# The seam between a long convolution and a gated MLP: v kept in DRAM by chunks, loads and side work reordered

## The chip, the core and the metric

The kernel runs on one core of one Trainium2 chip. Its engines are TensorE (PE in the profile; PEld is its weight load), VectorE (DVE), ScalarE (ACT), GpSimd (POOL) and SyncE (SP), each with its own in-order list of instructions, and 16 DMA engines that they share. SP issues nearly all loads, POOL nearly all stores and the copies between buffers. The metric is the device time of one execution in microseconds (us); a time of a kernel is the median of several executions. In this document a time within the execution, such as 457.14, is counted in us from the start of the span.

## The reference, cut to what matters

The inputs are 2048 tokens of 576 channels. Two blocks follow each other, each with a layer norm in front and a residual around it (sa, ca, ga, sb, cb, gb come from a small conditioning product):

```
h = layernorm(x) * (1 + ca) + sa
x = x + ga * A(h)          # A: a state-space layer as a long causal convolution
h = layernorm(x) * (1 + cb) + sb
x = x + gb * B(h)          # B: a gated MLP

A: K[d, l] = Re sum_n C[d,n] * exp(dt*A[d,n]*l) * dt*B[d,n];  y = causal_conv(u, K) + u * Dskip
B: z = gelu(x @ w_in);  z1, z2 = halves of z;  z2 = layernorm(z2)
   g = w_sp @ z2 + b_sp;  out = (z1 * g) @ w_out
```

## The kernel before

**Convolution.** The convolution is done as a transform in stages of small matmuls. The 576 channels are cut into five chunks: four of 128 and one of 64 (`CHW`); the code calls the last two `c3` and `c4`. Per chunk the stages are `u_unit` (forward), `z_unit` (multiply by the transformed kernel), `v_unit` (inverse, first half) and `y_unit` (inverse, second half, plus the residual). A unit of u, z or v is 128 partitions by 512 values; a chunk of 128 channels has eight, the last chunk four. Between `v_unit` and `y_unit` the data change their layout by way of DRAM: `v_unit` lets ACT copy ("evict") its PSUM result to an SBUF tile `v` (two buffers), and POOL stores that to `v_d`; `y_vload` loads two halves of four token tiles back with SP, `y_xload` loads the same piece of the input x, `y_unit` multiplies, DVE adds PSUM and x in place, and POOL stores the sum to `x1_d`. There are 4 y units per chunk, numbered 0 to 3. Tiles of the names "u1", "ue", "us", "za", "zb" are used again, once their first use is over, as places for these loads. A loop over ticks interleaves all this with the making of the kernel K; it ends before the last chunks are through.

**The seam** (lines 652 to 701) is written out by hand, and its order is kept on each engine as written (`mlp.nc = mlp.tied`). It mixes the last z, v and y units with the start of the MLP: 

- `start` loads `mrow` (the two modulation rows), `x1l` (the last chunk's 64 channels of x) and part of `x1f` (the first four token tiles of x); `start_load(q)` loads block q of the gate half of `w_in` (five blocks of 512 columns; 0 and 1 were loaded in the loop).
- Each block is turned into two fp16 parts: `start_sum(q)` lets ACT sum the squares, `win_scale` has PE add these over partitions and DVE make a power of two of it (seven small instructions), `start_hi(q)` converts on ACT, `start_lo(q)` makes the remainders with three DVE instructions and frees the block's buffer.
- `start_rows` bounds the modulation rows: two squares on ACT, a maximum on DVE, a scale (`pow2_scale`), the scaling of `mrow`, a one-value Gelu that loads ACT's table ahead of time, and the product INV_IN of three scales.
- `ln2_stats`, `roots` and `ln2_rows` make the second layer norm of a token tile on DVE.

**The MLP's first phase** (`phase_a`, line 1077) goes over 16 token tiles. `turn` transposes the normed tile on PE into PSUM, `turn_hi` copies it to fp16 on ACT, `turn_lo` makes the remainder on DVE and stores `nt`; `z2_mm(b, h)` is 14 matmuls of tile b with block h. In the first tile blocks 3 and 4 are still being prepared: `start_sum(3)`, `win_scale(8)`, `start_hi(3)`, `start_lo(3)` and the same for block 4 stand between the first matmul groups. The second phase (`phase_b`) makes the other half of z, the gate and the output.

**Queues.** Each DMA takes one of eight semaphores of its queue in turn, and so waits until the DMA eight places before it on that queue has landed. An SP or POOL instruction that waits holds up all behind it.

Line 129 stands in the profile for everything that went through the recording layer (the seam and `phase_a`), so in these stretches instructions are told apart by their tiles: `wz<-wst` on ACT with 2560 values is a sum of squares, with 2048 a conversion; `wz` on DVE is a split; `xb`, `us`, `zhl` and `x1l` on DVE with `pk` are y sums (`zhl` holds `x1f`).

Of the kernel before, what the change touches and what calls it, by code (L numbers as in the profile page):

```python
# [141 lines left out]
def ssm(tc, I, x1_d, consts_s, dram, mod_d, mlp):  # L142
# [5 lines left out]
    with ExitStack() as ctx:  # L148
# [3 lines left out]
        early = ctx.enter_context(ExitStack())  # L152

        u1_d = dram.tile([2, 16, 128, D], F32, name="u1_d")
        v_d = dram.tile([128, 32, D], F32, name="v_d")
        pa_d = dram.tile([4, 6, CW], BF, name="pa_d")
        pb_d = dram.tile([4, 6, CW], BF, name="pb_d")
        pc_d = dram.tile([4, 3, CW], BF, name="pc_d")
# [294 lines left out]
        def chan(c):  # L453
            return slice(CH0[c], CH0[c] + CHW[c])
# [40 lines left out]

        def v_unit(c, i):
            za, zb = st.pop((c, i))
            v = part("v")
            pm = ps1()
            T.matmul(pm, inva, za, start=True, stop=False)  # L500
            T.matmul(pm, invb, zb, start=False, stop=True)
            A.activation(v, pm, AF.Copy)
            G.dma_start(v_d[:, kr(c, i), chan(c)], by(v, c))

        def y_vload(c, q):
            bs = slice(4 * q, 4 * q + 4)
            w = CHW[c]
            if c == NC - 1:
                t = part("ue", 4)
                vt = [t[:, :4 * w], t[:, 4 * w:]]  # L510
            elif c == NC - 2 and q < 2:
                vt = [part("za"), part("zb")]
            else:
                vt = [part("u1", 5)[:, :4 * w] for _ in range(2)]
            st["yv", c, q] = vt
            for hh in range(2):
                S.dma_start(by(vt[hh], c), v_d.rearrange("(b g r) k d -> b (g r k) d", g=4, r=2)[bs, 128 * hh:128 * hh + 128, chan(c)].rearrange("b p d -> p b d"))

        def y_xload(c, q):
            bs = slice(4 * q, 4 * q + 4)  # L520
            if c >= NC - 2 and q == 0:
                xb = mlp.x1f[:, :, chan(c)]
            elif c == NC - 1:
                xb = mlp.x1l[:, bs]
# [128 lines left out]
        mlp.nc = mlp.tied  # L653
        V, A, G, T, S = mlp.nc.vector, mlp.nc.scalar, mlp.nc.gpsimd, mlp.nc.tensor, mlp.nc.sync
        c3, c4 = NC - 2, NC - 1
        y_load(2, 2)
        mlp.start()
        mlp.start_load(2)
        mlp.start_x1()
        for i in range(2):  # L660
            z_unit(c4, i)
# [2 lines left out]
        for i in range(2):  # L664
            z_unit(c4, 2 + i)
            v_unit(c4, i)
            mlp.win_scale(5 + i, False)
            if i == 0:
                mlp.start_sum(1)
        v_unit(c4, 2)  # L670
        v_unit(c4, 3)
        for c, r in ((2, 3), (c3, 0), (c3, 1), (c3, 2), (c3, 3), (c4, 0), (c4, 1), (c4, 2), (c4, 3)):
            y_xload(c, r)
        y_unit(2, 1)
        for c, r in ((2, 3), (c3, 0), (c3, 1), (c4, 0), (c4, 1)):
            y_vload(c, r)
        mlp.start_hi(0)
        mlp.start_hi(1)
        mlp.start_lo(0)
        y_unit(2, 2)  # L680
        y_vload(c3, 2)
        mlp.start_sum(2)
        mlp.win_scale(7, False)
        mlp.start_lo(1)
        y_unit(2, 3)
        y_vload(c3, 3)
        y_vload(c4, 2)
        y_vload(c4, 3)
        mlp.start_hi(2)
        mlp.start_rows(ps2(), ps2())  # L690
        mlp.start_lo(2)
        y_unit(c3, 0)
        mlp.start_load(3)
        y_unit(c4, 0)
        mlp.ap = mlp.mc
        mlp.ln2_stats(0)
        y_unit(c3, 1)
        mlp.roots(x=0)
        for c, r in ((c4, 1), (c3, 2), (c4, 2), (c3, 3), (c4, 3)):
            y_unit(c, r)  # L700
        mlp.nc = tc.nc

# [43 lines left out]
class Mlp:  # L746
# [73 lines left out]
    def start(self):  # L820

        nc = self.nc
        V, S, I = nc.vector, nc.sync, self.I
        mc = self.mc = self.pool(self.ctx, "mc", 1)
        self.c2 = ExitStack()
        ones = self.ones = mc.tile([128, 128], F32, name="ones")
        V.memset(ones, 1.0)
        self.ident = mc.tile([128, 128], F32, name="ident")
        S.dma_start(self.ident, I["c_small"][:, :128])
        self.sc = mc.tile([128, 96], F32, name="sc")  # L830
        wzp = self.pool(self.c2, "wzp", 1)
# [3 lines left out]
        self.x1l = wzp.tile([128, 16, CHL], F32, name="x1l")  # L835
        S.dma_start(self.x1l[:, 4:], I["x"][:, 4:, D - CHL:])
# [9 lines left out]
    def start_rows(self, *ps):  # L846

        V, A, col, mrow = self.nc.vector, self.nc.scalar, self.col, self.mrow
        s0, s1 = [p[:, :, :D // 2] for p in ps]
        halves = [mrow[:, i].rearrange("p (h d) -> p h d", h=2) for i in range(2)]  # L850
        A.activation(s0, halves[0], AF.Square, accum_out=col(T0))
        A.activation(s1, halves[1], AF.Square)
        V.tensor_reduce(col(T1), s1, axis=mybir.AxisListType.XY, op=ALU.max)
# [5 lines left out]
        for q in range(5, 8):  # L859
            V.tensor_tensor(self.wcol(q, INV_IN), self.wcol(q, I_W), col(I_H), op=ALU.mult)  # L860

    def start_load(self, q, pool=None):
        n = min(512, FH - 512 * q)
# [119 lines left out]
    def ln2_stats(self, b):  # L983
        V, ap = self.nc.vector, self.ap
        if b < 4:
            self.xts[b] = self.x1f[:, b]
        else:
            V.tensor_copy(self.xts[b][:, D - CHL:], self.x1l[:, b])
# [88 lines left out]
    def phase_a(self):  # L1077
# [313 lines left out]
```

## Time and profile before

| | |
|---|---|
| median of 3 runs | 1921.5 us (1918.57 to 1923.9) |
| profiled execution | 1920.97 us, span 1919.2 us |
| PE busy | 1814.3 us, 95% of the span |
| DVE busy | 908.5 us, 47% |
| ACT busy | 636.4 us, 33% |
| POOL busy | 207.9 us, 11% |
| data moved by DMA | 290.42 MB, mean 151 GB/s |
| mean granted PE clock | 0.981 |

How to read what follows. A row of the timeline has the start in us, the duration in us, the engine (a q behind it: its sequencer, which issues), the line, the operation, the tiles as out<-in, shapes, how many instructions were merged, and in brackets the idle time of the engine before it with what ended that. An instruction's end is its start plus its duration, and on DVE and ACT the next may start a little before that. A row of a tile's view has the count, the durations in ns, and the first and last start; "DMA to landing" is the time from issue to the last byte. In a table of stretches each engine has its busy us and its instructions; then come the granted PE clock, the mean busy share of the DMA engines (over 1 where transfers overlap) and GB/s.

### The profile page before, as it was taken

To read this page: it belongs to the slowest core of one execution; us is meant where nothing else is said; L and a number is where in the kernel's file an instruction comes from. 1 tells how busy PE (TensorE), PEld (TensorE's weight loads), DVE (VectorE), ACT (ScalarE), POOL (GpSimd) and SP (SyncE) were. 2 spreads that over 40 slices of the span, in tenths; PEclk is the share of its full clock that TensorE was granted. 3 is DMA by queue.
4 is the path that set the end of the run, shared out by engine and by line. 5 is a ranking of instruction groups with operands and counts; after the bars stand their busy time and mean duration, and the time that the engine had idled before them with its cause. 6 is when DMAs were issued, how large, how long until landed. Compare 5 with 4: busy or idle time off the path is not lost.

```text
span 1919.2 us, 28165 instructions
## 1 busy us (share of the span) xinstructions
PE 1814.3 (95%) x11634; PEld 934.3 (49%) x11634; DVE 908.5 (47%) x2020; ACT 636.4 (33%) x874; POOL 207.9 (11%) x317
## 2 busy tenths in 40 slices
PE   3778999986999998999999999999999999999999
PEld 1444555654444443444466444457444447444457
DVE  5987999848999871224352121152212143211221
ACT  3768999743777552121100011110101110001000
POOL 3121223331121110000000000000000000000000
PEclk9888999997999999999999999999999999999999
DMA  8667546897565456446552233452323342223211
GB/s 218 171 176 252 133 130 169 199 273 219 188 235 188 147 185 241 165 168 212 195 176 72 87 116 121 182 179 68 108 94 137 131 174 67 105 88 114 73 59 38
DMA packets 144145, 290.42 MB, mean 151 GB/s; under 512 B 20912, under 2 KB 74672, under 8 KB 133648
## 3 DMA queue, kind: packets, MB, share of 16 engines
q1 hardware_dynamic: 111888, 141.58, 24.0%
q0 software_dynamic: 29824, 142.47, 22.2%
q10 hardware_dynamic: 2304, 4.57, 0.6%
q8 instruction: 91, 1.49, 0.3%
q14 instruction: 38, 0.31, 0.1%
HBM read 219.11 MB, written 60.02 MB: 145 GB/s over the span
## 4 chain that ended last, share of the span: by engine, by line
PE 67%; DVE 7%; issue 4%; ACT 3%; DMA 2%; POOL 1%; DVEq 0%; ACTq 0%; POOLq 0%
PE pg L1233 13%; PE pg L1234 13%; PE pg L1235 13%; PE pz L1221 11%; PE pz L129 4%; PE po L1267 3%; PE po L1268 3%; PE po L1269 3%; DVE bsz L129 1%; ACT zhl L129 1%; DMA wsst<-in_w_spT 1%; PE po L1221 1%; DMA wf<-win_d 1%; PE pk L491 1%; DVE nt L129 1%
## 5 line engine op out<-in xcount | busy, mean ns | idle before, releaser
L1233 PE MATMUL pg<-wsp,z2f 128*128 128x512 f16 x1152 | 437.2, 380 | 0.0
L1234 PE MATMUL pg<-wsp,z2f 128*128 128x512 f16 x1152 | 436.6, 379 | 0.0
L1235 PE MATMUL pg<-wsp,z2f 128*128 128x512 f16 x1152 | 436.6, 379 | 0.0
L1237 DVE SCALAR_TENSOR_TENSOR gt<-pg,sc,bsp 128x512 f32<-128x512 f32 x72 | 54.0, 750 | 632.9 <-PE pg L1235 632.9
L1241 ACT ACTIVATE z<-gt 128x512 f16<-128x512 f32 x72 | 45.3, 630 | 802.7 <-DVE gt L1239 802.7
L129 PE MATMUL pz<-wz,nt 128*128 128x512 f16 (+1 forms) x1120 | 240.4, 363 | 5.5 <-DVE nt L129 2.3
L1221 PE MATMUL pz<-n2q,wf 128*128 128x512 f16 (+1 forms) x924 | 219.5, 383 | 4.2 <-DMA wf<-win_d 4.2
L1233 PEld LDWEIGHTS <-z2f 128*128 128x128 f16 x1152 | 112.6, 98 | 142.2 <-issue 13.6
L1235 PEld LDWEIGHTS <-z2f 128*128 128x128 f16 x1152 | 112.7, 98 | 135.9
L1234 PEld LDWEIGHTS <-z2f 128*128 128x128 f16 x1152 | 112.7, 98 | 128.6
L129 PEld LDWEIGHTS <-nt 128*128 128x128 f16 x1120 | 105.2, 99 | 136.7 <-issue 45.6
L1221 PEld LDWEIGHTS <-wf 128*128 128x128 f16 x1008 | 98.0, 98 | 147.1 <-issue 35.0
L1268 PE MATMUL po<-wout,z 128*128 128x288 f16 x576 | 164.7, 286 | 0.2 <-DVE ot L1271 0.2
L1267 PE MATMUL po<-wout,z 128*128 128x288 f16 x576 | 164.8, 286 | 0.0
L1269 PE MATMUL po<-wout,z 128*128 128x288 f16 x576 | 164.7, 286 | 0.0
L1229 POOL DMA_DIRECT2D z2f<-z_d x72 | 38.7, 537 | 1071.7 <-PE pg L1235 998.0
L1270 ACT ACTIVATE ot<-po 128x288 f32<-128x288 f32 x32 | 13.1, 410 | 194.2 <-PE po L1267 187.6
L1271 DVE TENSOR_TENSOR ot<-ot,po 128x288 f32<-128x288 f32 x32 | 14.5, 453 | 131.8 <-ACT ot L1270 131.7
L1242 DVE TENSOR_TENSOR gt<-gt,z 128x512 f32<-128x512 f32 x72 | 49.7, 690 | 45.6 <-ACT z L1241 45.6
L1267 PEld LDWEIGHTS <-z 128*128 128x128 f16 x576 | 56.4, 98 | 14.9 <-issue 0.7
L1269 PEld LDWEIGHTS <-z 128*128 128x128 f16 x576 | 56.4, 98 | 14.6 <-issue 0.4
L1268 PEld LDWEIGHTS <-z 128*128 128x128 f16 x576 | 56.4, 98 | 14.2
(283 smaller groups left out, 2404.5 us busy)
## 6 DMA issues: line engine op xcount, KB each, us to landing
z2f<-z_d POOLq DMA_DIRECT2D x72, 1024.0 KB, 5.1
wsst<-in_w_spT SPq DMA_DIRECT2D x64, 512.0 KB, 4.5
wf<-win_d SPq DMA_DIRECT2D x72, 320.0 KB, 3.2
z_d<-zhl POOLq DMA_DIRECT2D x16, 1152.0 KB, 6.8
u_d<-st1o POOLq DMA_DIRECT2D x16, 576.0 KB, 4.3
u<-u_d SPq DMA_DIRECT2D x36, 256.0 KB, 4.8
us<-ue POOLq DMA_DIRECT2D x72, 128.0 KB, 4.5
v_d<-v POOLq DMA_DIRECT2D x36, 256.0 KB, 3.7
```

The lines of the kernel that those rows point to most:

```text
L129: return self.tc.keep_in_program_order(f(*a, **k))
L1221: nc.tensor.matmul(pm.rearrange("p (t c) -> p t c", t=4), w[:p, kw], self.n2[q][:p, :, kn], start=i == 0, stop=i == len(Z1) - 1)
L1229: nc.gpsimd.dma_start(z2, self.z2_d[f])
L1233: T.matmul(pm, z2[:, st, 0], w[:, 0], start=st == 0, stop=False)
L1234: T.matmul(pm, z2[:, st, 0], w[:, 1], start=False, stop=False)
L1235: T.matmul(pm, z2[:, st, 1], w[:, 0], start=False, stop=st == 15)
L1237: V.scalar_tensor_tensor(t, pm, self.qcol(q, INV_SP), self.bsp[q], op0=ALU.mult, op1=ALU.add)
L1241: A.activation(p[:, 0], t, AF.Copy)
L1242: V.tensor_tensor(t, t, p[:, 0], op=ALU.subtract)
L1267: T.matmul(pl[:, :288], p[:, 1, ts], self.wout[:, f, 0, hs], start=f == 0, stop=f == 17)
L1268: T.matmul(pa[:, :288], p[:, 0, ts], self.wout[:, f, 0, hs], start=f == 0, stop=False)
L1269: T.matmul(pa[:, :288], p[:, 0, ts], self.wout[:, f, 1, hs], start=False, stop=f == 17)
```

## The change

Four things change, all around the seam.

1. `v_d` becomes five DRAM tensors, one for each chunk, with the chunk's channels innermost. A partition of a `v` tile is then one run of 2 KB in DRAM (before: runs of 512 bytes, 256 in the last chunk). The loads read the same number of bytes in runs of the same length as before.
2. The last two v units write their evictions to tiles of the name "ue" (four buffers). The x load of y unit (2, 2) is issued after the loads of w_in block 2. Block 0's conversion stands ahead of the last two v units, block 1's after them; the splits of blocks 0 and 1 stand ahead of and between the first y units. The load of block 3 keeps its place on SP.
3. `start_rows` is divided: its two squares (`start_sums`) come early, the rest after y unit (2, 2) and ahead of the sum of squares of block 2, which now comes behind the table load on ACT; INV_IN of block 2 is made in `win_scale(7)`, which moves behind y unit (2, 3). The split of block 2 moves into `phase_a`, between `turn_hi(0)` and `turn_lo(0)`, and frees its buffer for the load of block 4 there.
4. `ln2_rows(0)` stands ahead of the last four y units instead of behind them. `x1l` loses its unused first four rows.

```diff
-        v_d = dram.tile([128, 32, D], F32, name="v_d")
+        v_d = [dram.tile([128, 32, w], F32, name="v_d") for w in CHW]
...
         def v_unit(c, i):
             za, zb = st.pop((c, i))
-            v = part("v")
+            v = part("ue", 4) if c == NC - 1 and i > 1 else part("v")
...
-            G.dma_start(v_d[:, kr(c, i), chan(c)], by(v, c))
+            G.dma_start(v_d[c][:, kr(c, i)], by(v, c))
...
+            rows = v_d[c].rearrange("(b h g) k d -> b h (g k) d", b=16, h=2)[bs].rearrange("b h p d -> p h b d")
...
-                S.dma_start(by(vt[hh], c), v_d.rearrange("(b g r) k d -> b (g r k) d", g=4, r=2)[bs, 128 * hh:128 * hh + 128, chan(c)].rearrange("b p d -> p b d"))
+                S.dma_start(by(vt[hh], c), rows[:, hh])
...
-        y_load(2, 2)
+        y_vload(2, 2)
         mlp.start()
         mlp.start_load(2)
+        y_xload(2, 2)
         mlp.start_x1()
...
+        mlp.start_hi(0)
         v_unit(c4, 2)
         v_unit(c4, 3)
...
+        mlp.start_hi(1)
+        mlp.start_lo(0)
         y_unit(2, 1)
...
-        mlp.start_hi(0)
-        mlp.start_hi(1)
-        mlp.start_lo(0)
+        mlp.start_sums(ps2(), ps2())
+        mlp.start_lo(1)
         y_unit(2, 2)
         y_vload(c3, 2)
+        mlp.start_rows()
         mlp.start_sum(2)
-        mlp.win_scale(7, False)
-        mlp.start_lo(1)
         y_unit(2, 3)
...
+        mlp.start_load(3)
+        mlp.win_scale(7)
+        y_unit(c3, 0)
+        y_unit(c4, 0)
         mlp.start_hi(2)
-        mlp.start_rows(ps2(), ps2())
-        mlp.start_lo(2)
-        y_unit(c3, 0)
-        mlp.start_load(3)
-        y_unit(c4, 0)
         mlp.ap = mlp.mc
         mlp.ln2_stats(0)
         y_unit(c3, 1)
         mlp.roots(x=0)
-        for c, r in ((c4, 1), (c3, 2), (c4, 2), (c3, 3), (c4, 3)):
+        y_unit(c4, 1)
+        mlp.ln2_rows(0)
+        for c, r in ((c3, 2), (c4, 2), (c3, 3), (c4, 3)):
             y_unit(c, r)
...
+    def start_sums(self, *ps):
+        A, mrow = self.nc.scalar, self.mrow
+        s0, self.sq = [p[:, :, :D // 2] for p in ps]
+        halves = [mrow[:, i].rearrange("p (h d) -> p h d", h=2) for i in range(2)]
+        A.activation(s0, halves[0], AF.Square, accum_out=self.col(T0))
+        A.activation(self.sq, halves[1], AF.Square)
...
         V.tensor_scalar(mrow, mrow, col(S_H), None, op0=ALU.mult)
+        for q in range(5, 7):
+            V.tensor_tensor(self.wcol(q, INV_IN), self.wcol(q, I_W), col(I_H), op=ALU.mult)
         A.activation(col(T0), self.ones[:, :1], AF.Gelu_apprx_tanh)
...
             if b == 1:
                 self.ln2_stats(1)
                 self.roots(x=1)
-            self.ln2_rows(b)
+                self.ln2_rows(1)
             if b == 0:
                 self.turn(0)
                 self.turn_hi(0)
+                self.start_lo(2)
                 self.start_load(4)
                 self.x1_load(4)
                 self.turn_lo(0)
```

More of the change, by code (lines that the diff above doesn't have):

```diff
@@ L507, in y_vload @@
             w = CHW[c]
+            rows = v_d[c].rearrange("(b h g) k d -> b h (g k) d", b=16, h=2)[bs].rearrange("b h p d -> p h b d")
             if c == NC - 1:
                 t = part("ue", 4)
-                vt = [t[:, :4 * w], t[:, 4 * w:]]
-            elif c == NC - 2 and q < 2:
+                st["yv", c, q] = t[:, :4 * w], t[:, 4 * w:]
+                for hh in range(2):
+                    S.dma_start(by(t[:, 4 * w * hh:4 * w * hh + 4 * w], c), rows[:, hh])
+                return
+            if c == NC - 2 and q < 2:
                 vt = [part("za"), part("zb")]
@@ L523, in y_xload @@
             elif c == NC - 1:
-                xb = mlp.x1l[:, bs]
+                xb = mlp.x1l[:, 4 * q - 4:4 * q]
             else:
@@ L834, in start @@
         self.wz = wzp.tile([128, 10, FH], F16, name="wz")
-        self.x1l = wzp.tile([128, 16, CHL], F32, name="x1l")
-        S.dma_start(self.x1l[:, 4:], I["x"][:, 4:, D - CHL:])
+        self.x1l = wzp.tile([128, 12, CHL], F32, name="x1l")
+        S.dma_start(self.x1l, I["x"][:, 4:, D - CHL:])
         self.xz = self.pool(self.c2, "xz", 1)
@@ L844, in start_x1, with start_rows @@
         self.nc.sync.dma_start(self.x1f[:, :, :384], self.x1_d[:4, :, :384].rearrange("b p d -> p b d"))
-    def start_rows(self, *ps):
-        V, A, col, mrow = self.nc.vector, self.nc.scalar, self.col, self.mrow
[L849 to L853, printed above, removed]
+    def start_sums(self, *ps):
[4 more added lines that the diff above has]
+        A.activation(self.sq, halves[1], AF.Square)
+    def start_rows(self):
+        V, A, col, mrow = self.nc.vector, self.nc.scalar, self.col, self.mrow
+        V.tensor_reduce(col(T1), self.sq, axis=mybir.AxisListType.XY, op=ALU.max)
         V.tensor_scalar(col(T1), col(T1), 1152.0, None, op0=ALU.mult)
@@ L987, in ln2_stats @@
         else:
-            V.tensor_copy(self.xts[b][:, D - CHL:], self.x1l[:, b])
+            V.tensor_copy(self.xts[b][:, D - CHL:], self.x1l[:, b - 4])
         x = self.xts[b]
```

2 lines of the change are left out of this document (removed).

## The prediction

> **What bounds the kernel now.** I read the page first (PE busy 95% of the span, DVE 47%, DMA 0.9 and over in slices 8 and 9 alone), then cut the span where the change lies, at the seam between the convolution and the gated MLP. Columns: stretch, PE, PEld, DVE, ACT, POOL busy, granted clock, DMA share, GB/s.
>
> ```profile
> 405.00:430.00 25.00, 20.12 (x126) 13.80 (x124) 10.04 (x28) 10.85 (x12) 6.97 (x9) 0.95 1.05 315
> 430.00:457.00 27.00, 12.85 (x151) 11.73 (x151) 23.38 (x58) 8.66 (x11) 7.46 (x10) 0.69 1.02 297
> 457.00:480.00 23.00, 18.35 (x76) 8.14 (x77) 19.53 (x62) 10.04 (x14) 0.55 (x1) 0.87 0.41 137
> 480.00:700.00 220.00, 216.78 (x1067) 99.34 (x1064) 196.07 (x634) 148.16 (x185) 33.48 (x45) 1.00 0.59 195
> ```
>
> From 480 on PE is 98.5% busy: what happens there is a matter of when it starts. Between 430 and 457 PE works half of the time and DVE 87%; DMA is full from 405 to 457. So the seam is worth what DVE's in-order list there is worth, unless DMA holds it. The timeline at the end of the seam:
>
> ```profile
> 446.31 1.01 DVE L129 TENSOR_TENSOR zhl<-pk,zhl 128x512 f32<-128x512 f32 x2
> 447.04 1.97 PE L129 MATMUL pk<-u,st 128*64 128x128 f32 x16 [5.98 <-DVE zhl L129]
> 453.40 0.82 DVE L129 SCALAR_TENSOR_TENSOR n<-zhl,mvx,mrow 128x576 f32<-128x576 f32 x1
> 455.10 0.19 DVE L129 COPY n<-n 128x64 f32<-128x64 f32 x1
> 457.14 5.42 PE L129 MATMUL pz<-wz,nt 128*128 128x512 f16 x14 [0.69 <-ACT nt L129]
> 457.29 1.02 DVE L129 TENSOR_TENSOR nt<-pt,nt 128x512 f16<-128x512 f32 x2 [1.99 <-ACT nt L129]
> ...
> 469.38 0.38 PE L129 MATMUL pz<-acc,ones 128*128 128x1 f32 x2 [2.66 <-ACT wz L129]
> 478.59 6.12 PE L129 MATMUL pz<-wz,nt 128*128 128x256 f16 x24 [0.84 <-DVE wz L129]
> ```
>
> PE waits 5.98 us for the y sums on DVE. The first MLP matmul starts at 457.14, but PE then still waits for what hangs on DVE: at 469.38 for a sum of squares queued on ACT behind a conversion that needs a DVE scale, at 478.59 for DVE's last weight split. So I count to the place where DVE takes up `nt` (the low part of the first tile, 457.29): everything DVE does after it up to 478.59 is unchanged, and PE is chained to it. The end should move by what 457.29 moves by.
>
> **The change, part by part.** The chain starts on ACT and SP.
>
> ```profile
> 415.93 0.60 ACT L129 ACTIVATE v<-pk 128x512 f32<-128x512 f32 x1 [0.59 <-PE pk L129]
> 419.66 0.60 ACT L129 ACTIVATE v<-pk 128x512 f32<-128x512 f32 x1 [0.81 <-ACT wz L129]
> 424.88 0.60 ACT L129 ACTIVATE v<-pk 128x512 f32<-128x512 f32 x1 [4.62 <-DMA v_d<-v]
> 427.26 3.88 ACT L129 ACTIVATE wz<-wst,sc 128x2048 f16<-128x2048 f32 x2
> ```
>
> *Evictions of v into "ue", first conversion ahead of them.* The third v eviction of the last chunk waits 4.62 us for a store to free its buffer, and both conversions (1.94 us each, 3.88 for two) stand behind it. In the new order the first conversion follows the 419.66 eviction (some 0.5 later) and ends at 422.1 instead of 429.2; the two evictions have their own buffers.
>
> *Load of w_in block 2 in front of the x load.* SP's rows, and two v stores alone with their landing:
>
> ```profile
> 406.61 0.43 SPq L129 DMA_DIRECT2D x1l<-in_x  x1
> 413.31 0.37 SPq L129 DMA_DIRECT2D xb<-in_x  x1
> 414.29 2.66 SPq L129 DMA_DIRECT2D wst<-in_w_in  x3
> ...
> L129 POOL DMA_DIRECT2D v_d<-v x1: 762/762/762, 409.8 to 409.8; - x1
> ...
> DMA to landing us min/median/max: 5.6/5.6/5.6
> ...
> L129 POOL DMA_DIRECT2D v_d<-v x1: 896/896/896, 416.8 to 416.8; - x1
> ...
> DMA to landing us min/median/max: 8.0/8.0/8.0
> ```
>
> The x load waited until 413.31 for its buffer, and the zhl and w_in loads behind it on SP; now these go at about 407 and only the x load, the early x1 rows and the us loads are behind that wait. The price: the store issued at 409.8 (landed after 5.6, at 415.4) now stands behind the w_in load. The one store that stood so before (issued at 416.8, just behind the 414.29 load) took 8.0. The eviction at 415.93 reuses that buffer. At 5.6 it isn't held. At 8.0 it starts at 417.8; the sum of squares behind it ends 2.9 later (415.93 to 419.66-0.81) at 420.7, the next eviction and the conversion add 0.5 and 1.9: the conversion ends at 423.15. I take 422.6, the middle of two near ends. The Trainium skill, "DMA: Bandwidth & Descriptors", section "Queues, rings and completion order", says that a DMA engine takes turns between queues a packet at a time. By that rule the POOL store would not wait for SP's load, the conversion would end at 422.1 and the time come out 0.5 lower; the 8.0 above speaks against it.
>
> *DVE and the row sums.* The rows that give the steps:
>
> ```profile
> 429.29 2.35 DVE L129 SCALAR_TENSOR_TENSOR wz<-wst,sc,wz 128x2048 f16<-128x2048 f32 x1 [4.26 <-ACT wz L129]
> 432.74 0.68 DVE L129 TENSOR_TENSOR xb<-pk,xb 128x512 f32<-128x512 f32 x1
> 439.57 0.74 DVE L129 TENSOR_REDUCE sc<-ps 128x1 f32<-128x576 f32 x1
> 440.77 1.28 ACT L129 ACT_TABLE_LOAD   x1 [2.24 <-DVE sc L129]
> 442.06 0.20 ACT L129 ACTIVATE sc<-ones 128x1 f32<-128x1 f32 x1
> ...
> 431.05 2.32 ACT L129 ACTIVATE wz<-wst 128x2560 f16<-128x2560 f32 x1
> 433.51 0.58 PE L129 MATMUL pk<-acc,ones 128*128 128x1 f32 x2 [8.38 <-ACT wz L129]
> 434.03 1.97 PE L129 MATMUL pk<-u,st 128*64 128x128 f32 x16
> 434.13 0.16 DVE L129 COPY sc<-pk 128x1 f32<-128x1 f32 x1 [0.72 <-PE pk L129]
> 435.53 2.34 DVE L129 SCALAR_TENSOR_TENSOR wz<-wst,sc,wz 128x2048 f16<-128x2048 f32 x1
> ```
>
> A weight split is three DVE instructions, 3.45 us to the next (429.29 to 432.74); a y sum 0.68. New list from the conversion's end: 0.1, split 0, sum, split 1, sum: 8.36, so the row maximum starts at 430.96 (before 439.57). The two squares it needs are ACT's next work and long done. Then comes a new serial loop: the table load waits for DVE 1.20 after the maximum's start, it and the dummy take 1.49, and the third sum of squares is now queued behind them (ACT): 433.65. From its start to PE's matmul 2.46, to 436.11; behind that matmul on PE stands y sum (chunk 4, first), whose matmuls start 0.52 later and take 1.97: 438.6. DVE comes first with its scale: 0.62 to the copy, 1.40 for the seven small ones, 0.16 for the product that moved here: 438.29. During this loop DVE idles some 2 us, which the old order did not. The first zhl sum starts at 438.7 instead of 446.31: 7.6 earlier.
>
> From there to the end of the first tile's norm it was 446.31 to 455.29: 8.98, now in another order but the same instructions; 0.2 more because the second sum's matmuls (half of those 1.97) end a little after the first sum. Split 2 (3.45) comes after, so DVE takes up `nt` at 438.7+0.2+8.98+3.45 = 451.3. The 1.99 us in which DVE waited for transposes and ACT is covered: the norm is done before the last four sums, and PE and ACT turn the tile under split 2. So 457.29 becomes 451.3: 6.0 us earlier.
>
> *Loads of v.* The last must not be later than DVE.
>
> ```profile
> 433.59 3.13 SPq L129 DMA_DIRECT2D ue<-v_d  x4
> ...
> L129 POOL DMA_DIRECT2D v_d<-v x2: 885/885/885, 425.8 to 427.7; - x2
> ...
> DMA to landing us min/median/max: 5.6/5.7/5.8
> ...
> L129 SPq DMA_DIRECT2D ue<-v_d x4: 465/798/1060, 439.7 to 442.2; - x4
> ...
> DMA to landing us min/median/max: 5.5/5.9/6.5
> ```
>
> They were released at 433.59 by the landing of the last v store (issued 427.7, in 5.8); the last, issued at 442.2, landed by 447.7 (5.5 to 6.5). The last v eviction now comes at about 424 and its store at 425, so 2.7 us earlier, and the last load by 445.0. The last sum stood 0.7 (itself and a memset) ahead of 453.40, so 6.4 after 446.31; with the norm (453.40 to 455.29) now in front it comes at 438.7+0.2+6.4+1.9 = 447.2, so it is covered by about 1.5.
>
> *2-KB stores* I cost at nothing: the last chunk's stores in runs of 256 B landed in 5.6 to 5.8 beside 5.6 for one in runs of 512 B, under the same full DMA, so the run length doesn't show. Bounds: 0 to 0.3 us on the last store. The later load of w_in block 4, now issued when split 2 ends at 451, lands within 9 us and is needed about 12 later. The smaller x1l and the fewer scale products are nothing.
>
> **Sum.** Profiled execution 1920.97 (span 1919.2 and 1.8 around it) less 6.0 is 1915.0; it lies 0.5 below the median of 1921.5, so the forecast for a median is 1915.5. Half a us of it hangs on the store, up or down.
>
> **Rivals.**
> 1. *The w_in load starves the stores.* If the 409.8 store lands only with all the traffic ahead of it, at about 420 (10.2 us, over the 8.0 row), the conversion ends at 425.4 and 2.8 of the 6.0 are gone: 1918.3. For it: DMA is full. Against: the load is no longer behind another 6 us of loads.
> 2. *DMA sets the last sum.* If the v loads land no earlier than before (447.7), then matmuls 0.65, the sum 0.45, a memset 0.3 and split 2 put `nt` at 452.7: 1916.9. For it: the share of 1.02. Against: DMA isn't asked for more, and starts earlier.
> 3. *Larger gain.* The store isn't held, DVE's 2-us wait in the loop is filled: 8 us, 1913.5.
> 4. *Slower.* A store's rows now lie 16 KB apart (32x128x4 bytes), where they were 72 KB apart. If such writes collide in DRAM, all 36 stores land later.
>
> ```profile
> v_d<-v POOLq DMA_DIRECT2D x36, 256.0 KB, 3.7
> 400.73 0.78 POOL L503 DMA_DIRECT2D v_d<-v  x1 [3.52 <-ACT v L502]
> ```
>
> A v buffer returns after two stores, 9.1 us (400.73 to 409.8); a store takes 3.7. It decides from about 9 us a store; each us over that costs some 14 us over 14 pairs, so at 9.9 the gain is lost twice: 1928. The trace shows no pitch effect, so 5%. The Trainium skill, same page, section "Latency and other measured facts", has rates falling with large power-of-two row pitches (207 GB/s at 512 KiB, 103 at 4 MiB). By that rule 16 KiB is far below where it starts, and even half the rate would keep a store under 9 us; no run here shows it yet.
>
> **How the numbers follow.** A difference under 0.3% (5.8 us) is about what a measurement of this kernel can't tell from no change, so the bound for "faster" is 1915.7. The forecast case has 0.55, with its own range 1913.5 to 1917; I put 0.40 of it below the bound; its centre lies just under that, and the 2 us of waiting that I charge in the loop may be less. Larger gain 0.12. Starved stores 0.14 and late loads 0.10 fall within 0.3%. Slower 0.09: the pitch 0.05, an unseen wait 0.04. Faster 0.52, same 0.39, slower 0.09. The range 1911.5 to 1920.0 leaves out the slower cases and part of the largest gain.
>
> **What would show it.** Right: the first two weight conversions on ACT near 420 to 426 without a wait for v_d; w_in block 2 issued near 407.5; the row maximum on DVE near 431; the zhl sum near 438.7; `nt` on DVE near 451, the transposes some 3 us before; the stretch from there to the end unchanged. Wrong: an ACT wait for v_d ahead of the 415.93 eviction of more than 2 us; PE waiting for v loads at the last sums; DVE waiting more than 3 us between the row maximum and the zhl sum; v stores landing in over 9 us in the loop.

## The result

The changed kernel takes 1917.4 us at the median (1910.9 to 1922.2), the kernel before, beside it on the same chip, 1922.1 us. The ratio is 0.9975, with a 95% interval of 0.9967 to 0.9984: about 5 us, or 3 to 6, inside the 0.3% that the forecast had called no measurable change. The profiled execution took 1917.79 us (span 1916.0), where the forecast's own sum for it was 1915.0.

The stretches of the changed kernel, columns as in the forecast (stretch, PE, PEld, DVE, ACT, POOL busy, granted clock, DMA share, GB/s):

```profile
405.00:430.00 25.00, 20.65 (x136) 14.17 (x132) 16.16 (x34) 13.09 (x15) 5.68 (x10) 0.96 1.10 335
430.00:457.00 27.00, 20.05 (x168) 14.98 (x169) 21.11 (x63) 9.30 (x10) 8.06 (x11) 0.60 0.97 284
457.00:480.00 23.00, 17.76 (x75) 7.76 (x74) 19.99 (x61) 9.70 (x12) 0.55 (x1) 0.85 0.55 180
480.00:700.00 220.00, 215.78 (x1064) 98.76 (x1062) 196.05 (x629) 148.43 (x189) 34.13 (x45) 1.00 0.58 194
```

DVE's work has moved ahead of 430 (16.16 us where it was 10.04), DMA is still full from 405 to 457, and behind 480 these sums show no change.

**One number for all traces.** The seam's first eviction of v (unit (c3, 6)) starts at different times in different executions of the same code ahead of it, so every trace is read from that eviction; it is called the mark below. Here it is in the kernel before and in the changed kernel, with the long matmul group of `phase_a` that follows a wait for `nt`:

```profile
408.93 0.60 ACT L129 ACTIVATE v<-pk 128x512 f32<-128x512 f32 x1 [5.10 <-PE pk L129]
...
702.60 13.00 PE L129 MATMUL pz<-wz,nt 128*128 128x512 f16 x62 [0.65 <-DVE nt L129]
```

```profile
409.46 0.60 ACT L129 ACTIVATE v<-pk 128x512 f32<-128x512 f32 x1 [5.10 <-PE pk L129]
...
699.33 13.00 PE L129 MATMUL pz<-wz,nt 128*128 128x512 f16 x62 [0.66 <-DVE nt L129]
```

From mark to `nt` on DVE (457.29 before, 453.98 after) it is 48.36 and 44.52: 3.84 gained. From `nt` to this group it is 245.31 and 245.35, and from the group to the end of the span 1216.60 and 1216.67. In these two traces all of the gain lies between mark and `nt`. The forecast had 6.0 there.

The timeline of the changed kernel, ACT and DVE. First the part that came as foretold:

```profile
420.38 0.60 ACT L129 ACTIVATE v<-pk 128x512 f32<-128x512 f32 x1 [1.00 <-DMA v_d<-v]
420.87 1.99 ACT L129 ACTIVATE wz<-wst,sc 128x2048 f16<-128x2048 f32 x1
423.80 0.60 ACT L129 ACTIVATE ue<-pk 128x512 f32<-128x512 f32 x1 [0.45 <-PE pk L129]
430.99 0.74 DVE L129 TENSOR_REDUCE sc<-ps 128x1 f32<-128x576 f32 x1
435.51 0.69 DVE L129 TENSOR_TENSOR us<-pk,us 128x512 f32<-128x512 f32 x1 [1.22 <-PE pk L129]
436.68 0.16 DVE L129 COPY sc<-pk 128x1 f32<-128x1 f32 x1 [0.48 <-PE pk L129]
438.60 0.69 DVE L129 TENSOR_TENSOR zhl<-pk,zhl 128x512 f32<-128x512 f32 x1 [0.24 <-PE pk L129]
```

The first conversion starts 6.4 earlier than before, the wait of 4.62 for a store is one of 1.00, the row maximum stands at 430.99 and the first zhl sum at 438.60. The second part did not:

```profile
441.67 1.04 PE L129 MATMUL pk<-u,st 128*64 128x128 f32 x16
444.98 0.44 PE L129 MATMUL pk<-ue,st 128*64 128x64 f32 x2 [2.27 <-DVE n L129]
445.98 1.01 PE L129 MATMUL pk<-ue,st 128*64 128x64 f32 x13 [0.55 <-DMA ue<-v_d]
446.89 1.91 PE L129 MATMUL pk<-u,st 128*64 128x128 f32 x15
447.13 0.42 DVE L129 TENSOR_TENSOR x1l<-pk,x1l 128x256 f32<-128x256 f32 x1 [0.58 <-PE pk L129]
448.39 1.27 PE L129 MATMUL pk<-ue,st 128*64 128x64 f32 x16
448.84 0.69 DVE L129 TENSOR_TENSOR us<-pk,us 128x512 f32<-128x512 f32 x1 [1.28 <-PE pk L129]
450.53 2.35 DVE L129 SCALAR_TENSOR_TENSOR wz<-wst,sc,wz 128x2048 f16<-128x2048 f32 x1
453.98 1.00 DVE L129 TENSOR_TENSOR nt<-pt,nt 128x512 f16<-128x512 f32 x2
```

PE stands 2.27 and then 0.55 in front of y unit (c4, 2). The first wait is put down to DVE's `n`, which has nothing to do with these matmuls; the first half of (c4, 2)'s data, issued at 439.21, landed after 5.6 us at 444.85, just ahead of them. The second wait names the load. Behind them on PE stand (c3, 3), whose data are long there, and (c4, 3); DVE waits 0.58 and 1.28 for their sums. The loads on SP's queue, and the view of the last four (the row of the issues and the time to landing):

```profile
424.54 2.85 SPq L129 DMA_DIRECT2D u<-v_d  x2
427.56 0.60 SPq L129 DMA_DIRECT2D za<-v_d  x1
428.25 1.91 SPq L129 DMA_DIRECT2D zb<-v_d  x1
430.21 0.75 SPq L129 DMA_DIRECT2D za<-v_d  x1
431.01 0.71 SPq L129 DMA_DIRECT2D zb<-v_d  x1
431.96 3.84 SPq L129 DMA_DIRECT2D ue<-v_d  x4
435.89 3.22 SPq L129 DMA_DIRECT2D u<-v_d  x4
439.21 3.17 SPq L129 DMA_DIRECT2D ue<-v_d  x4
```

```profile
L129 SPq DMA_DIRECT2D ue<-v_d x4: 612/672/1013, 439.2 to 441.4; - x4
...
DMA to landing us min/median/max: 5.6/5.9/6.1
```

In the kernel before SP stood until 433.59 for a store to land. Now it waits for nothing that long: it issues one load after the other, each issue lasting 0.5 to 2.1 us. The last four are issued from 439.2 to 441.4 (before 439.7 to 442.2) and the last lands at 447.1, where the forecast had 445.0.

### The profile page after: what moved, and what is told of

It reads as the page before. It is cut to its first block, busy times and chain, and to the rows that moved or that the text cites. A ratio compares the mean times of both kernels' runs of the same rounds, so it can differ in the third digit from the quotient of the medians.

```text
span 1916.0 us, 28166 instructions
## 1 busy us (share of the span) xinstructions
PE 1817.7 (95%) x11634; PEld 935.4 (49%) x11634; DVE 908.1 (47%) x2020; ACT 636.3 (33%) x874; POOL 199.5 (10%) x317
## 4 chain that ended last, share of the span: by engine, by line
PE 69%; DVE 7%; issue 3%; ACT 3%; DMA 1%; SPq 0%; DVEq 0%; ACTq 0%
PE pg L1244 13%; PE pg L1245 13%; PE pg L1246 13%; PE pz L1232 11%; PE po L1278 4%; PE po L1280 4%; PE po L1279 4%; PE pz L129 2%; ACT zhl L129 1%; PE pk L129 1%; DVE bsz L129 1%; DVE nt L129 1%; PE po L1232 1%; PE pk L478 1%; PE pk L491 1%
```

## The experiments

Times in this table are counted from the mark of each trace. The ratio is to the kernel before, with its 95% interval; kernels without a ratio were executed once.

| kernel | mark | first conversion | first zhl sum | nt | from zhl sum to nt | ratio |
|---|---|---|---|---|---|---|
| before | 408.93 | 18.33 | 37.38 | 48.36 | 10.98 | |
| before, once more | 410.27 | 18.36 | 37.41 | 48.39 | 10.98 | |
| changed | 409.46 | 11.41 | 29.14 | 44.52 | 15.38 | 0.9975 (0.9967 to 0.9984) |
| without three x loads | 411.88 | 11.62 | 30.45 | 43.11 | 12.66 | |
| (c3, 3) ahead of (c4, 2) | 410.09 | 11.64 | 29.36 | 42.44 | 13.08 | 0.9963 (0.9951 to 0.9974) |
| that, split 2 in the seam | 411.93 | 11.45 | 29.17 | 42.25 | 13.08 | 0.9960 (0.9947 to 0.9973) |
| sum 2 ahead of the row bound | 413.30 | 11.63 | 27.26 | 43.97 | 16.71 | 0.9977 (0.9968 to 0.9986) |
| evictions back in v | 410.52 | 11.56 | 32.49 | 45.52 | 13.03 | 0.9984 (0.9974 to 0.9993) |
| x load first again | 412.53 | 11.23 | 28.95 | 44.62 | 15.67 | 0.9988 (0.9978 to 0.9998) |
| norm last again | 413.82 | 11.53 | 29.25 | 45.48 | 16.23 | 0.9992 (0.9981 to 1.0004) |
| before, v_d by chunks alone | 412.02 | 18.37 | 37.42 | 48.39 | 10.97 | 0.9999 (0.9989 to 1.0008) |
| before, evictions to ue alone | 410.47 | 11.23 | 34.09 | 45.08 | 10.99 | 0.9992 (0.9982 to 1.0002) |
| changed, waits filled | 409.38 | 11.38 | 30.21 | 39.53 | 9.32 | 0.9956 (0.9941 to 0.9971) |

From `nt` to the group of 62 matmuls all of them have 245.29 to 245.68. The gain at `nt` that a trace shows lies inside the interval of every ratio (the changed kernel: 3.84, interval 3.1 to 6.3 us).

**Is it DMA?** The x loads of three y units are left out, and POOL writes zeros there.

```diff
                 xb = by(part("us", 4) if c == NC - 2 or (c, q) == (2, 3) else part("xb"), c)
-                S.dma_start(xb, I["x"][:, bs, chan(c)])
+                if c < NC - 2:
+                    S.dma_start(xb, I["x"][:, bs, chan(c)])
+                else:
+                    G.memset(xb, 0.0)
```

> The changed kernel, where the x loads of y units (c3, 1) to (c3, 3), 256 KB each, are left out and POOL writes zeros into these tiles instead (so three sums lack x). Theory (DMA sets the last sums): at some 310 GB/s these 0.75 MB are 2.4 us of a full DMA, the last v loads of the last chunk land at 444.5 to 445.5 instead of 447.1, PE's waits of 2.27 and 0.55 in front of (c4, 2) shrink to under 1 us, and DVE takes up nt at 451.5 to 452.5 instead of 453.98. Rival (the order on SP and PE sets them, not the bytes): the loads land within 0.5 of 447.1 and nt stays at 453.5 or later.

The view of the last four loads of v, and the DVE and POOL rows of the split behind the first conversion:

```profile
L129 SPq DMA_DIRECT2D ue<-v_d x4: 577/770/1235, 438.4 to 440.7; - x4
...
DMA to landing us min/median/max: 4.6/4.8/5.3
```

```profile
427.63 1.47 POOL L129 MEMSET us<- 128x512 f32 x3
```

```profile
427.80 1.59 DVE L129 TENSOR_SCALAR wz<-wst,sc 128x512 f16<-128x512 f32 x1
```

The last load is issued 28.8 behind the mark (31.9 in the changed kernel) and lands 33.4 to 34.1 behind it (37.5 to 38.0): 3.4 to 4.6 earlier, more than the 2.4 us of its bytes. PE no longer waits for (c4, 2), and zhl sum to `nt` takes 12.66, not 15.38; the forecast's terms for it, 9.18 and 3.45, make 12.63. So what stands ahead of the last loads of v on SP's queue does set them. The run takes away both the bytes and SP's time to issue these x loads (the last load of v is issued 3.1 earlier, and then lands 0.8 to 1.0 sooner), so it doesn't tell the two apart. Counted from the changed kernel's mark, `nt` would stand at 452.57, just past the edge of what was expected, since the zeros cost something else: the DVE instruction beside POOL's memsets took 1.59 us where it takes 0.48, and the whole list up to the zhl sum is 1.3 late.

**Is it PE's order too?** The sums that wait stand ahead of one that doesn't; then the split is put into the gap as well.

```diff
-        for c, r in ((c3, 2), (c4, 2), (c3, 3), (c4, 3)):
+        for c, r in ((c3, 2), (c3, 3), (c4, 2), (c4, 3)):
             y_unit(c, r)
```

> The changed kernel, with y unit (c3, 3) in front of (c4, 2). Theory (late loads of the last chunk, and PE in order behind them): (c3, 3)'s matmuls and sum fill the wait, the last sum starts some 1.2 earlier (at 448.5), nt at 452.8 instead of 453.98; against the kernel before 0.9969. Rival (the forecast's view, DVE's list alone sets nt): no change of nt by more than 0.3, 0.9975.

`nt` comes at 42.44, 2.08 earlier than in the changed kernel, with a ratio of 0.9963. PE still waits for the loads here, for both halves of (c4, 3), the last unit.

```profile
446.33 0.30 PE L129 MATMUL pk<-ue,st 128*64 128x64 f32 x2 [0.43 <-DMA ue<-v_d]
447.09 0.68 PE L129 MATMUL pk<-ue,st 128*64 128x64 f32 x14 [0.46 <-DMA ue<-v_d]
```

The gain is larger than the 1.2 expected because DVE's waits behind the norm are all gone, and PE runs faster: 14 matmuls of (c4, 3) take 0.68 here, 16 took 1.27 in the changed kernel. The granted clock is 1.00 here; in the changed kernel it is 0.50 from 445.0 to 449.7, where the last three units run. What that costs can be read from the run below with the evictions back in `v`, which has the changed kernel's order and a clock of 1.00 in this place. Its rows of (c3, 3) and (c4, 3):

```profile
447.43 1.04 PE L129 MATMUL pk<-u,st 128*64 128x128 f32 x15
448.56 0.69 PE L129 MATMUL pk<-ue,st 128*64 128x64 f32 x16
```

The changed kernel has 1.91 and 1.27 for the same matmuls. From the third matmul of (c4, 2), the first that waited for the second load, to the end of (c4, 3) it takes 3.68, and that run 2.33: 1.35 for the clock. So the loss had three parts: loads later than thought, PE's units in order behind the first of them, and a clock of 0.50 for these units. This run changes the last two together and doesn't separate them. They may hang together: in the changed kernel the clock is 0.98 from 444 to 445 and 0.50 from 445 to 446, so it falls as PE takes up (c4, 2) after standing for 2.27. It was 0.50 there too in the three other runs in which PE stood over 1.5 us in this place (2.48, 2.15 and 1.55), and 1.00 in this run, without the x loads and with the evictions back in `v`, where no wait there reaches 1 us. In the run shown next, with waits of 0.87 and 0.57, it falls in the last unit: 1.00 from 449 to 450, 0.71 to 451, 0.50 to 452. That the standing brings it down was not tested.

```diff
-        for c, r in ((c3, 2), (c4, 2), (c3, 3), (c4, 3)):
-            y_unit(c, r)
+        y_unit(c3, 2)
+        y_unit(c3, 3)
+        mlp.start_lo(2)
+        y_unit(c4, 2)
+        y_unit(c4, 3)
...
                 self.turn_hi(0)
-                self.start_lo(2)
```

> As the run with (c3, 3) first, and the split of block 2 (3.45 us of DVE) also goes back into the seam, behind the sum (c3, 3) and in front of the sums (c4, 2) and (c4, 3). Theory: DVE splits while the last loads land, so its waits of 0.58, 1.28 and 0.16 behind the norm are gone: nt at 452.0 instead of 453.98, the end 2.0 earlier than the changed kernel's, 0.9965 of the kernel before. Rival (something behind nt holds PE, the load of block 3 say): nt earlier but the last matmul group of the first tile as late as in the changed kernel, 0.9975.

42.25, 0.9960: `nt` is as early as expected, but the run before has nearly all of it already (42.44). With (c3, 3) first DVE had no wait left there for the split to fill.

**Was it the loop on ACT?** The forecast had charged some 2 us of waiting between the row maximum and the zhl sum.

```diff
-        mlp.start_rows()
         mlp.start_sum(2)
+        mlp.start_rows()
```

> The changed kernel, with the sum of squares of block 2 in front of the row bound's rest, so ACT does it at 427.5 and not behind the table load. The loop of the forecast (1.22 and 0.48 of waiting on DVE) goes: first zhl sum at 437.6 or earlier instead of 438.6. Theory (the last loads set nt): nt within 0.4 of 453.98 all the same, ratio 0.9975. Rival (DVE's chain from the row maximum sets it): nt 1.0 or more earlier, 0.9970.

The first zhl sum comes 1.88 earlier, `nt` only 0.55, between the two and nearer to the theory. What is saved in front is waited for behind:

```profile
442.54 0.42 DVE L129 TENSOR_TENSOR zhl<-pk,zhl 128x256 f32<-128x256 f32 x1 [1.29 <-PE pk L129]
450.41 0.42 DVE L129 TENSOR_TENSOR x1l<-pk,x1l 128x256 f32<-128x256 f32 x1 [1.21 <-PE pk L129]
452.12 0.69 DVE L129 TENSOR_TENSOR us<-pk,us 128x512 f32<-128x512 f32 x1 [1.28 <-PE pk L129]
```

**One part undone.** First the evictions:

```diff
-            v = part("ue", 4) if c == NC - 1 and i > 1 else part("v")
+            v = part("v")
```

> The changed kernel, with the last two evictions back in the two v buffers. Theory: the third and fourth eviction wait for stores that land at 424.3 and 427.1 there, conversion 1 starts at 427.7 instead of 424.29, split 1 and all of DVE's list behind it 3 us later, the last store and with it the loads of v (c4, 2), (c4, 3) 3 us later too: from the eviction that stands at 409.46 in the changed kernel to nt 47.5 instead of 44.52, ratio to the kernel before 0.9990. Rival (these evictions matter little, since DMA sets the loads of v): 44.5 to 45.5, ratio 0.9975 to 0.9980.

```profile
428.83 0.60 ACT L129 ACTIVATE v<-pk 128x512 f32<-128x512 f32 x1 [3.90 <-DMA v_d<-v]
```

The wait for the store is back, and the zhl sum is 3.35 later, as the theory said. But `nt` is only 1.00 later, at the rival's upper end: the list then arrives when the loads have landed (13.03 from zhl sum to `nt`, not 15.38), and PE's clock is 1.00 there. The last store of v is issued 4.0 later than in the changed kernel, counted from the mark, and yet the last load lands at 37.2, not later than 37.6 there: a release 4 us later does not make it land later.

```diff
-        y_vload(2, 2)
+        y_load(2, 2)
         mlp.start()
         mlp.start_load(2)
-        y_xload(2, 2)
```

> The changed kernel, with the x load of (2, 2) back in front of the loads of w_in block 2. Theory (DMA is full all along, so the order of the two changes nothing that nt hangs on; block 2's sum of squares stands at 433.6, 11 us behind the load's landing): eviction to nt 44.5 within 0.6, ratio 0.9975. The forecast's own view (the w_in load ahead holds the store, so conversion 0 is some 0.5 earlier here): 44.0. Rival (the earlier load of block 2 frees DMA for the loads of v): nt 1 us or more later, 0.9980 or more.

44.62 against 44.52: the order of the x load and block 2's load brings nothing at `nt`. The first conversion starts 0.18 earlier, so block 2's load ahead of the store costs ACT about 0.2 where the forecast had taken 0.5. The ratio of 0.9988 lies above the expected 0.9975; its interval reaches down to 0.9978, and this trace gives 3.7 us at the group of 62 matmuls (0.9981). Whether the order costs something that this one trace doesn't show stays open.

```diff
-        mlp.ln2_rows(0)
         for c, r in ((c3, 2), (c4, 2), (c3, 3), (c4, 3)):
             y_unit(c, r)
+        mlp.ln2_rows(0)
```

> The changed kernel, with the first tile's norm back behind the last four y sums. Theory (the norm's 1.9 us fill waits for the late v loads where they stand): without it DVE waits that much more in front of these sums, the norm comes after them, and the transposes and ACT's part of nt come behind it: eviction to nt 46.3 to 47.0 instead of 44.52, ratio 0.9985. Rival (split 2 covers it just as well): 44.5 to 45, 0.9977.

45.48, 0.96 later; 1.8 to 2.5 had been expected. That lies between theory and rival. The norm's 1.9 us fill the wait where the change puts them, but half of the gap is made up: at the end split 2 covers the transposes as before. The ratio, 0.9992, is above both expectations; its interval holds the 2.88 us of this trace (0.9985).

**One part alone.** The kernel before with the five tensors `v_d`, and the loads that go with them:

```diff
-        v_d = dram.tile([128, 32, D], F32, name="v_d")
+        v_d = [dram.tile([128, 32, w], F32, name="v_d") for w in CHW]
...
-            G.dma_start(v_d[:, kr(c, i), chan(c)], by(v, c))
+            G.dma_start(v_d[c][:, kr(c, i)], by(v, c))
...
+            rows = v_d[c].rearrange("(b h g) k d -> b h (g k) d", b=16, h=2)[bs].rearrange("b h p d -> p h b d")
...
-                S.dma_start(by(vt[hh], c), v_d.rearrange("(b g r) k d -> b (g r k) d", g=4, r=2)[bs, 128 * hh:128 * hh + 128, chan(c)].rearrange("b p d -> p b d"))
+                S.dma_start(by(vt[hh], c), rows[:, hh])
```

> The kernel before, with v_d by chunks alone (2-KB stores), nothing else moved. The time from the eviction of v that stands at 408.93 in the kernel before to DVE's nt (457.29, so 48.36) is the measure. Theory (stores cost nothing and bring nothing): 48.36 within 0.6, ratio 0.9995 to 1.0005; the wait of 4.62 for v_d stays over 4. Rival A (faster stores are a part of the gain): the wait under 3.5, the measure 47.3 or less, ratio 0.9993 or less. Rival B (16-KB pitch costs): stores land later than 6 us in the loop, the convolution longer, ratio 1.0015 or more.

48.39 against 48.36, ratio 0.9999: 2-KB stores and a pitch of 16 KB do nothing for the time. The third eviction still waits 3.91 for a store, a little under the 4 that was set, and the fourth another 2.04.

```profile
427.26 0.60 ACT L129 ACTIVATE v<-pk 128x512 f32<-128x512 f32 x1 [3.91 <-DMA v_d<-v]
429.90 0.60 ACT L129 ACTIVATE v<-pk 128x512 f32<-128x512 f32 x1 [2.04 <-DMA v_d<-v]
```

The kernel before with the two evictions alone:

```diff
-            v = part("v")
+            v = part("ue", 4) if c == NC - 1 and i > 1 else part("v")
...
+        mlp.start_hi(0)
         v_unit(c4, 2)
         v_unit(c4, 3)
...
-        mlp.start_hi(0)
         mlp.start_hi(1)
```

> The kernel before with one part of the change alone: the last two evictions of v into tiles of the name ue, and conversion 0 ahead of them. Theory (this part starts DVE's list some 6 us earlier, and the old list then runs into the late loads of v at its end): eviction to nt 43 to 45 against 48.36 before and 44.52 with the whole change, ratio 0.9970 to 0.9978: nearly the whole gain from this part. Rival (row sums and norm carry half of the gain): 46 or more, ratio 0.9985 or more.

45.08, just past the 43 to 45 expected: by the trace 3.28 of the change's 3.84 come from this part alone. Its ratio, 0.9992 with an interval of 0.9982 to 1.0002, is higher than expected; it holds the 3.28 us (0.9983) only near its lower end, so the timing by itself doesn't confirm it. Together with the run that undid the same part (45.52, so the rest brings 2.84 without it) it says that the parts don't add: 3.28 and 2.84 would be 6.12, and together they bring 3.84. This part alone doesn't meet the last loads, as the theory had it: zhl sum to `nt` is 10.99, as before. Its first conversion comes 7.1 earlier, and 3.8 of that is lost ahead of the zhl sum, where split 0 now stands behind the sum of (2, 1) on DVE and the sum of (2, 3) waits 1.80 for PE, which waited for its loads. Nor does the rest alone lose much at the end (13.03 for 12.63 of work). Only both together bring the list to the last units ahead of PE (15.38).

**The kernel before once more.**

> The kernel before once more, for how far its stretches vary from one execution to the next. Expected: the time of the eviction that stood at 408.93 anywhere from 408 to 414 (the runs so far have 409.46 to 413.82 for it, though no run changes what comes ahead of it), from it to nt 48.36 within 0.3, from nt to the 62-matmul group near 702 within 0.3 of 245.31.

The mark at 410.27, and from it 48.39; from `nt` to the group 245.34 (704.00). What varies from one execution to the next lies ahead of the mark (408.93 to 413.82 over all traces) and behind the group of 62 matmuls (1211.8 to 1216.7 to the end of the span); from mark to `nt` these two executions differ by 0.03.

**The waits filled.** Block 2's scale and conversion go ahead of the row bound, which so becomes work for the time in which (2, 3) waits for its loads; split 2 stands ahead of the zhl sums, (c3, 3) ahead of (c4, 2).

```diff
-        mlp.start_rows()
         mlp.start_sum(2)
+        mlp.win_scale(7, False)
+        mlp.start_hi(2)
+        mlp.start_rows()
         y_unit(2, 3)
+        mlp.start_lo(2)
...
-        mlp.win_scale(7)
         y_unit(c3, 0)
         y_unit(c4, 0)
-        mlp.start_hi(2)
...
-        for c, r in ((c3, 2), (c4, 2), (c3, 3), (c4, 3)):
+        for c, r in ((c3, 2), (c3, 3), (c4, 2), (c4, 3)):
...
-        for q in range(5, 7):
+        for q in range(5, 8):
...
-                self.start_lo(2)
```

> The changed kernel with its waits filled: block 2's sum of squares, scale and conversion in front of the row bound, so the row bound is DVE's work while y sum (2, 3) waits for its loads; block 2's split back in the seam, in front of the zhl sums; (c3, 3) in front of (c4, 2). Worked from the changed kernel's times: row bound 432.4 to 436, sum (2, 3), split 2 to 440.2, then 1.1 of zhl sums, 6.5 to the norm's end, four sums of 2.2 and a memset: nt at 449.8, so 40.4 from the eviction at 409.46 instead of 44.52. Theory (waits for late loads are what the change lost, work put there is free): 40 to 41.5, ratio to the kernel before 0.9955. Rival (DMA holds the last sums in any order): 42 or more, as in the run with (c3, 3) first, ratio 0.9963.

```profile
432.25 0.75 DVE L129 TENSOR_REDUCE sc<-ps 128x1 f32<-128x576 f32 x1
435.55 0.68 DVE L129 TENSOR_TENSOR us<-pk,us 128x512 f32<-128x512 f32 x1
436.15 2.34 DVE L129 SCALAR_TENSOR_TENSOR wz<-wst,sc,wz 128x2048 f16<-128x2048 f32 x1
439.59 1.01 DVE L129 TENSOR_TENSOR zhl<-pk,zhl 128x512 f32<-128x512 f32 x2
446.70 0.68 PE L129 MATMUL pk<-ue,st 128*64 128x64 f32 x14 [0.68 <-DMA ue<-v_d]
448.91 1.02 DVE L129 TENSOR_TENSOR nt<-pt,nt 128x512 f16<-128x512 f32 x2 [0.43 <-ACT nt L129]
```

39.53, better than the 40.4 worked out, 5.0 earlier than in the changed kernel and 8.8 earlier than before. 1913.65 us at the median, ratio 0.9956 (0.9941 to 0.9971): faster than the kernel before. Against the changed kernel the trace says 5.0 us; the intervals of the two ratios overlap by a little (0.9967 to 0.9971). DVE has no wait from the row maximum to `nt` but 0.43, and that is for the transposes; the last loads of v are what stands right ahead of them on PE, whose clock is 1.00 here. So the seam has come to both bounds: earlier loads would bring that 0.43, and the rest is DVE's list itself.

## Why the prediction was right, and where it was wrong

The median of 1917.4 lies in the forecast's range and is 1.9 above its 1915.5; the profiled execution is 2.8 above its sum. The larger chance, 0.52, was put on a gain of over 0.3%; measured is 0.25%, with an interval of 0.16 to 0.33%. The way of the gain and, roughly, its size came as forecast, but not the end of the seam, where one of the forecast's own signs of being wrong showed: PE waiting for v loads at the last sums. Step by step, with 0.53 to be added to a forecast time for the later mark:

- *Counting to `nt`* held: 245.31 and 245.35 behind it. PE's first MLP matmul came 5.5 earlier and then waited 5.24 where it had waited 2.66, so that only `nt` counted.
- *Evictions and first conversion* held: its end was put at 422.6, and came at 422.86. The three stores issued from 410.4 to 417.4 landed in 6.0 to 6.9, between the two ends of 5.6 and 8.0. The Trainium skill's rule that the weighing set against the row ("DMA: Bandwidth & Descriptors", "Queues, rings and completion order") would have had the conversion end at 422.1 in the forecast's count; the 422.33 measured there lies between it and the 422.6 taken.
- *Block 2's load* was said to issue at about 407.5. The load ahead of it took 2.62 to issue at 407.63, and the first part of the block went at 410.31. Nothing hung on it, as the run with the x load first shows.
- *Row maximum and loop* held, and came a little early: 430.99 for 430.96 and 438.60 for 438.7 are 0.5 and 0.6 earlier when the later mark is taken off. DVE waits 1.94 us in the loop for "some 2". Of this, 1.22 stands in front of the sum of (2, 3), whose loads were late; the loop on ACT would have taken the time anyway, as in the run with (c3, 3) first, where that sum came in time and DVE waits 1.66 for the scale.
- *From the zhl sum to the end of the sums, 8.98 + 0.2*, failed: 438.60 to 450.53 is 11.93, 2.75 more. The step that failed is *Loads of v*, "the last load by 445.0 ... covered by about 1.5". It had moved the loads by what their release moved, 2.7. But the release was no longer what they waited for: behind a full DMA the last was issued only 1.3 earlier, counted from the mark (31.9 against 33.2), and landed only 1.1 earlier (37.6 against 38.7). In all traces with the x loads it lands 36.7 to 38.7 behind the mark, whenever the last v is stored; without three of them at 33.4. Of the 2.75, 1.35 is PE's clock of 0.50 behind the wait, for which the forecast had no term; the other 1.4 is the late loads, with three units in order behind the first of them. How much the order costs by itself stays open, since the run that changed it also had the full clock.
- *Split 2*, 3.45, and the cover of the transposes held: 450.53 to 453.98, the transposes at 449.58.
- *2-KB stores at nothing* held for the time (48.39, ratio 0.9999), and with it fell the rival of the pitch. The reason given, that the length of a run doesn't show in a store's landing, did not hold (see the last section). *Block 4's late load* held: the 56 matmuls of blocks 3 and 4 run without a stall at 466.51, where there had been two of 1.01 and 0.84.

```profile
466.06 0.59 PE L129 MATMUL pz<-acc,ones 128*128 128x1 f32 x2 [5.24 <-ACT wz L129]
466.51 14.27 PE L129 MATMUL pz<-wz,nt 128*128 128x512 f16 x56
```

That the forecast's time came so close in spite of this is partly luck: the front of the seam was 0.6 better than forecast, and the step that failed cost nearly half of a gain of 6 in a range that left room for it. What happened is in kind the second rival, "DMA sets the last sum", which had 0.10. Its time, 1916.9, was nearer than the forecast's. Its terms add up to 452.55 for `nt`, not the 452.7 that it gives; measured is 453.45 without the later mark, 0.90 more. Nearly all of that is the last unit's matmuls, 1.30 from their start to the sum where 0.65 was taken, at the clock of 0.50. The row that spoke for this rival, a DMA share of 1.02, was read and set aside because the loads "start earlier"; on the full DMA here, 2.7 of earlier release came out as 1.1 of earlier landing.

## What to carry to other kernels

When a wait for a release goes away on a queue whose DMA is full, the next bound is the traffic ahead: work out the landing from what stands in front, not from the release. On in-order engines a late load delays all that stands behind it, so put what is ready ahead of it, and put independent work (here the row bound and a split) where the list waits. Before a gain is put down to an order, compare the granted clock of the same matmuls in both traces. Parts of a change that lead to the same late transfer don't add up: try each alone and each undone before crediting one.

## What the runs showed of the hardware

- A DVE TENSOR_SCALAR of 128x512 took 1.59 us while POOL wrote three tiles of 128x512 with zeros (427.63 to 429.10), and 0.48 otherwise; it ended 0.3 behind POOL's last memset. The Trainium skill, "SBUF — State Buffer", section "SBUF: two separate sides", says that GpSimd and VectorE share one pair of ports, which a GpSimd instruction, or a VectorE instruction in a mode that uses both pairs, holds as a whole while the other is blocked. The trace agrees with that if this TENSOR_SCALAR ran in such a mode, which no run here shows.
- The length of a run in DRAM showed in a v store, though not in the kernel's time. POOL's issue took 0.54 us for runs of 2 KB, against 0.76 for runs of 512 bytes and 0.90 for runs of 256 (the two stores that the forecast quotes of the kernel before). From issue to landing the median of all v stores is 3.3 to 3.5 us in the ten traces with runs of 2 KB and 3.7 to 3.8 in the three without; 0.2 of the difference is the issue itself. The row of the run with v_d by chunks alone, to be held against the row of 3.7 in the prediction:

```profile
v_d<-v POOLq DMA_DIRECT2D x36, 256.0 KB, 3.3
```

Under the full DMA of the seam single stores differ by more than that. The view of v_d in the changed kernel from 409 to 420:

```profile
L129 POOL DMA_DIRECT2D v_d<-v x3: 542/543/547, 410.4 to 417.4; - x3
...
DMA to landing us min/median/max: 6.0/6.4/6.9
```

- The same matmuls in the same order took PE 3.68 us at a granted clock of 0.50 (changed kernel) and 2.33 at 1.00 (evictions back in `v`).
- While DMA was full (a share of 1.11 from 407 to 411) the issue of one load held SP for 2.62 us at 407.63, with no wait on record for it; at 405.64 one took 0.36.
- The time of the mark, and with it part of the spread of each kernel's times, varies from 409.38 to 413.82 between executions of the same code ahead of it. Most of it comes from the first 155 us: the last token tile of the first layer norm starts at 149.6 with the mark at 409.38, and at 154.5 with the mark at 413.30; from there to the mark it is 257.8 to 259.8 over all traces. What varies there stays open.
